# Turning the attention's tiles in two row tiles of 64 tokens, each with a PSUM bank of its own

## The chip, the cores and the metric

One Trainium2 chip, one of its cores. The time is the device time of one launch in microseconds (us). The kernel's engines are called PE (TensorE, with PEld for its weight loads), DVE (VectorE), ACT (ScalarE), POOL (GpSimd) and SP (SyncE, which only issues transfers here).

## What is computed

For 2048 tokens of width 448 the reference mixes two branches, token by token, with a gate `g`. Branch A is linear attention with 16 heads of 28; branch B sends each token to two of eight experts.

```python
g = sigmoid((x * gate_w).sum(-1))
# A
q, k, v = split(x @ wqkv)                              # 16 heads of 28
phi_q = concat(softmax(q @ w_phi), softmax(-(q @ w_phi)))   # 56 per head; phi_k alike
kv, z = phi_k^T v, sum(phi_k)
a = concat_heads(phi_q kv / (phi_q z + 1e-6)) @ wo
# B
top 2 of x @ w_gate -> gates;  b = sum over the two: gate * (silu(x @ w1[e]) @ w2[e])
out = g * a + (1 - g) * b
```

## The kernel before

The tokens are cut into 16 tiles `t` of 128. A first stage (to about 113 us) makes the values, the key maps and the state `kv` of all tiles, and routes the tokens. The stage that the change touches runs from 113 to 217 us: a loop over `t = 0 .. 17`, in which tile `t` is attended, tile `t + 2` prepared, tile `t - 1` turned, tile `t - 2` projected, and the queries of tile `t + 7` asked for. After it the experts run on PE to the end.

Order on PE, DVE and ACT is that of the program; on POOL nearly every instruction is chained behind the one before it (`in_turn`). One round `t` issues, in this order:

- POOL: three scatters of routing records (`store`, L475, in rounds 2 to 6, fewer in others), each allowed once tile `t` is attended; from round 8 on gathers of the first expert's tokens (L796) instead. Then `drop` (L586: queries' exponents less their maximum), `weigh`'s sum `om(t)` (L906) and the copy of its last 64 columns (L908). From round 9 on, a rearrangement of gathered tokens (L855).
- PE: `attend(t)` (L885, 64 matmuls in four tiles of 64x64, output `n` in the one pair of banks "T"); `flip(t + 2)`: the 128 x 1024 map of the queries is turned by eight full transposes (L712, `et`), the maps' tile `t + 2` being attended two rounds later; `project(t - 2)` (11 matmuls of 448 columns, `ao`); `turn(t - 1)`: the tile's output `om` of 128 x 512 is turned by four full transposes (L915, `ot`); `ask(t + 7)` (11 matmuls, `pq`, up to round 8); in rounds 10 to 14 `first_tokens` turns one tile of the first expert's tokens by four transposes (L860, `xgt`).
- DVE: `tops` (L581, maxima of the queries; in rounds 10 and 11 it stands behind `weigh` instead); `weigh(t)` (L895 to L901, ending in `w`, which also frees the banks of `n`); the rest of `turn(t - 1)` (L139, L140, which make `oh`, `ol`); the rest of `first_tokens` (L828, L829).
- ACT: signs and exponential of queries, the two copies of `et` (L713), the row's output `aos` (L925), `oh` (L137), `xgh` (L824).

PSUM has eight banks: "A" two (`pq`, `ao`), "T" two as one pair, "O" four in rotation (`et`, `ot`, `xgt`, and the routing's `pp`). `route(1)`, a routine that routes the second half of the tokens, advances by some steps at the head of each round; its matmuls into `pp` (L452, L454) are issued in round 1 and what reads them (L458 to L470) in round 2. L470 makes the addresses of the scatters that begin in round 2.

Of the kernel before, what the change touches and what calls it, by code (L numbers as in the profile page):

```python
# [8 lines left out]
F32 = mybir.dt.float32  # L9
# [3 lines left out]
AF = mybir.ActivationFunctionType  # L13
ALU = mybir.AluOpType
AX = mybir.AxisListType
PSUM = bass.MemoryType.PSUM
DRAM = bass.MemoryType.DRAM

P = 128
# [6 lines left out]
NT = S // P  # L26
# [36 lines left out]
LANDING = ("x00", "w0", "x10", "x20", "x30", "w1", "x01", "x40", "x11", "x50", "x21", "w2", "x31", "w3", "x41", "x51")  # L63
PIECES = ("00", "10", "20", "30", "01", "40", "11", "50", "21", "02", "12", "22", "31", "41", "03", "13", "23",
          "32", "51", "42", "52", "33", "43", "53")
BANKS = {"A": 2, "O": 4}
XLP = range(3, 16)
QBUFS = 5
ASKS = {9: 0, 10: 1, 11: 2, 12: 3, 14: 4}
# [2 lines left out]
NJ = 8  # L72
# [10 lines left out]
def gated_mix(ctx: ExitStack, tc: tile.TileContext, xt, xq, wk, wq, wv, wphi, wo, w12, out):  # L83
    nc = tc.nc
# [2 lines left out]
    cst = ctx.enter_context(tc.tile_pool(name="cst", bufs=1))  # L87
    dram = ctx.enter_context(tc.tile_pool(name="dram", bufs=1, space=DRAM))
    ps = ctx.enter_context(tc.tile_pool(name="ps", bufs=1, space=PSUM))

    def bank(tag, name):
        return ps.tile([P, 512], F32, tag=tag, name=name, bufs=BANKS[tag])

    def two_banks(name):
        return ps.tile([P, NJ, P], F32, tag="T", name=name, bufs=1)

    def after(i, others):
        for o in others:
# [37 lines left out]
    def xsplit(xh, xl, src, eng):  # L136
        nc.scalar.activation(xh, src, AF.Copy)  # L137
        lo = xh[64:P, 3]
        for i in (eng.tensor_tensor(out=lo, in0=src[64:P, 3], in1=lo.bitcast(F32), op=ALU.subtract),  # L139
                  eng.tensor_tensor(out=xl, in0=src[:, 0:3], in1=xh[:, 0:3].bitcast(F32), op=ALU.subtract)):  # L140
            if eng is nc.gpsimd:
                in_turn(i)
# [74 lines left out]
    ident = cst.tile([P, P], F32, name="ident")  # L217
# [10 lines left out]
    for what in LANDING:  # L228
        t = int(what[1])
# [41 lines left out]
    for t in range(NT):  # L271
        pool = pe if t < NT // 2 else px
# [3 lines left out]
    for n, m in (("k", D), ("v", VG), ("q", D), ("o", D)):  # L276
        pool = px if n in "qo" else pb
# [9 lines left out]
    half = [slice(64 * a, 64 * a + 64) for a in range(2)]  # L287
# [65 lines left out]
    for what in LANDING:  # L353
        t = int(what[1])
# [3 lines left out]
        c = FIRST[int(what[2])]  # L358
# [38 lines left out]
    def route(r):  # L397
        n = GROUPS[r + 1] - GROUPS[r]

        def tl(shape, name, dt=F32):  # L400
            return pr.tile([P] + shape, dt, tag=name, name=f"{name}{r}")

        tt, ts_ = nc.vector.tensor_tensor, nc.vector.tensor_scalar
        ts = slice(GROUPS[r], GROUPS[r + 1])
        b3 = [P, n, E]

        def wide(x):
            return x.unsqueeze(2).to_broadcast(b3)

        def each(x):  # L410
            return x.unsqueeze(1).to_broadcast(b3)


        def highest(l, m, sel):
            t = tl([n, E], "t")
            f = tl([n], "f")
            nc.vector.tensor_reduce(out=m, in_=l, axis=AX.X, op=ALU.max)
            tt(out=t, in0=l, in1=wide(m), op=ALU.is_equal)
            tt(out=t, in0=t, in1=each(down), op=ALU.mult)
            yield  # L420
            nc.vector.tensor_reduce(out=f, in_=t, axis=AX.X, op=ALU.max)
            tt(out=sel, in0=each(down), in1=wide(f), op=ALU.is_equal)

        l8 = L[:, ts, 0:E]
        g = gt[:, ts]
        omg, m1, m2 = tl([n], "omg"), tl([n], "m1"), tl([n], "m2")
        sel = [tl([n, E], f"sel{k}") for k in range(2)]
        l2 = tl([n, E], "l2")
        selb = tl([n + 1, E], "selb", BF16)
        nc.scalar.activation(g, L[:, ts, 8], AF.Exp, scale=-1.0)  # L430
        yield from highest(l8, m1, sel[0])
        nc.vector.scalar_tensor_tensor(out=l2, in0=sel[0], scalar=-3e38, in1=l8, op0=ALU.mult, op1=ALU.add)
        yield
        yield from highest(l2, m2, sel[1])
        nc.vector.memset(selb[:, n], 0.0)
        tt(out=selb[:, 0:n], in0=sel[0], in1=sel[1], op=ALU.add)
        tt(out=m2, in0=m2, in1=m1, op=ALU.subtract)
        yield
        nc.scalar.activation(m2, m2, AF.Exp)
        nc.vector.tensor_scalar_add(g, g, 1.0)  # L440
        nc.vector.reciprocal(g, g)
        ts_(omg, g, -1.0, 1.0, op0=ALU.mult, op1=ALU.add)
        yield
        nc.vector.tensor_scalar_add(m1, m2, 1.0)
        nc.vector.reciprocal(m1, m1)
        tt(out=rec[:, ts, 0, 1], in0=m1, in1=omg, op=ALU.mult)
        tt(out=rec[:, ts, 1, 1], in0=rec[:, ts, 0, 1], in1=m2, op=ALU.mult)
        yield
        pp = bank("O", f"pp{r}")
        nn = (n + 1) * E  # L450
        pos_p = pp[:, 0:nn].rearrange("p (t e) -> p t e", e=E)
        nc.tensor.matmul(pp[:, 0:nn], before, selb.rearrange("p t e -> p (t e)"), start=True, stop=False)  # L452
        for t in range(n):
            nc.tensor.matmul(pos_p[:, t + 1:], ones_b, selb[:, t:t + 1, :].to_broadcast([P, n - t, E]),  # L454
                             start=False, stop=t == n - 1)
        yield
        pos = tl([n + 1, E], "pos")
        tt(out=pos, in0=pos_p, in1=base.unsqueeze(1).to_broadcast([P, n + 1, E]), op=ALU.add)  # L458
        nc.vector.tensor_copy(base, pos[:, n])
        pos = pos[:, 0:n]  # L460
        slot = tl([n, E], "slot")
        s1 = tl([n, E], "s1")
        tt(out=slot, in0=pos, in1=each(kst), op=ALU.add)
        yield
        slot_f = tl([n, 2], "slot_f")
        slot_i = pr.tile([P, n, 2], I32, name=f"slot_i{r}")
        for k in range(2):
            tt(out=s1, in0=sel[k], in1=slot, op=ALU.mult)
            nc.vector.tensor_reduce(out=slot_f[:, :, k], in_=s1, axis=AX.X, op=ALU.add)
        nc.vector.tensor_copy(slot_i, slot_f)  # L470
        stores.extend((slot_i[:, t, k:k + 1], rec[:, ts.start + t, k, :]) for t in range(n) for k in range(2))
# [117 lines left out]
    def lower(e, n, pool):  # L589
        drop(e, tops(e, n, pool))  # L590
# [74 lines left out]
    for t in range(NT):  # L665
# [19 lines left out]
        if 1 <= t < 5:  # L685
            c = t - 1
# [16 lines left out]

    et = {}

    def flip(t):
        et[t] = pt.tile([P, NJ, P], F32, tag="et", name=f"et{t}", bufs=2)
        e = EQ[t].rearrange("p h f -> p (h f)")
        for a in range(0, NJ, 4):
            tp = bank("O", f"et{t}{a}")  # L710
            for j in range(4):
                nc.tensor.transpose(tp[:, j * P:(j + 1) * P], e[:, (a + j) * P:(a + j + 1) * P], ident)  # L712
            nc.scalar.activation(et[t][:, a:a + 4], tp.rearrange("p (a n) -> p a n", n=P), AF.Copy)  # L713
# [16 lines left out]
    b = blocks(kvs)  # L730
# [120 lines left out]
    def first_tokens(c):  # L851
        m = P if c < nm else EX
        t = xg[0, c][0:m]
        x4 = pm.tile([P, 4, 4, 32], F32, tag="xt", name=f"x40{c}")[0:m]
        in_turn(nc.gpsimd.tensor_copy(x4, t.rearrange("p a (c k) -> p c a k", c=4)))  # L855
        yield
        tp = bank("O", f"xgt0{c}")
        v = tp[:, 0:4 * m].rearrange("p (c n) -> p c n", c=4)
        for i in range(4):
            nc.tensor.transpose(v[:, i], x4[:, i].rearrange("p a k -> p (a k)"), ident[0:m, 0:m])  # L860
        if c == 0:
            xg[0] = (pw.tile([P, 4, CAP], F32R, tag="xgh", name="xgh0", bufs=1),
                     pw.tile([P, 3, CAP], F32R, tag="xgl", name="xgl0", bufs=1))
        at = slice(c * P, c * P + m)
        both(xg[0][0][:, :, at], xg[0][1][:, :, at], v)
# [6 lines left out]
    om, oh, ol = {}, {}, {}  # L872
# [34 lines left out]
                                        in0=w5[:, :, :, 0], in1=w5[:, :, :, 1], op=ALU.add))  # L907
        in_turn(nc.gpsimd.tensor_copy(o[:, D:512], o[:, 384:D]))  # L908

    def turn(t):  # L910
        oh[t] = pc.tile([P, 4, P], F32R, tag="oh", name=f"oh{t}")
        ol[t] = pc.tile([P, 3, P], F32R, tag="ol", name=f"ol{t}")
        tp = bank("O", f"ot{t}").rearrange("p (c n) -> p c n", n=P)
        for c in range(4):
            nc.tensor.transpose(tp[:, c], om[t][:, c * P:(c + 1) * P], ident)  # L915
        xsplit(oh[t], ol[t], tp, nc.vector)

    def project(t):
        o = bank("A", f"ao{t}")
# [244 lines left out]
    def fill_in():  # L1164
        n = len(fill)
        fill.append((*FILL[n // 2], n % 2))
        first(*fill[-1])

    def part_way():
        for g in list(coming):  # L1170
            if next(g, 0) == 0:
                coming.remove(g)

    at, k = None, 0
    for t in range(NT + 2):
        u = t + QAHEAD
# [22 lines left out]
        k = t - (NT if at is None else at)  # L1199
# [7 lines left out]
            weigh(t, n_)  # L1207
        if u < NT and not early_top:
            lower(EQ[u], f"q{u}", pr)
        if t + 2 < NT:  # L1210
            flip(t + 2)
        if t >= 2:
            if t == NT + 1:
                fill_in()
            leave_row(t - 2, project(t - 2))
        if t == NT:
            fill_in()
        if 1 <= t <= NT:
            turn(t - 1)
        if t in QASKS:  # L1220
            ask(QASKS[t], some=(0 if t else 5, 11))
        if t == NT - 1:
# [16 lines left out]
        if SPLIT <= t < SPLIT + 3 and splits:  # L1239
            if next(splits[0], 0) == 0:  # L1240
                del splits[0]
                if splits:
                    next(splits[0])
    assert not coming and not splits
    runs["on"] = False
    pc_stack.close()
    px_stack.close()
# [14 lines left out]
    for s in range(E * NFC):  # L1262
        e, fc = divmod(s, NFC)
        k, i = divmod(s, 2)
# [26 lines left out]
        n = 3 * nm  # L1291
        if e == E - 1 and fc > NFC - LATE:
            n = n // 2 if fc < NFC - 1 else 0
        if fc % 2 == 0:
            f = first_pair(e, fc // 2)
# [7 lines left out]
    with tc.manual_schedule(engines={mybir.EngineType.PE}):  # L1303
        last = reached["pe"]
        for cs in ((0, 1), (2,), (3,)):
            for at in (0, 2):
                for c in cs:
                    for i in range(2):
                        share(E - 1, NFC - LATE + at + i, c, last)
                    if at:  # L1310
                        leave(E - 1, (c,))
    pf_stack.close()


    loads, (n_ov,) = nc.values_load_multi_w_load_instructions(nov_i[0:1, 0:1], min_val=0, max_val=MAXOV)  # L1315
# [98 lines left out]
```

## Time and profile before

| | |
|---|---|
| three runs | 789.95, 790.08, 791.45 us; median 790.08 |
| the profiled execution | 790.2 us, its span 788.2 us (2.0 us lie around the span) |
| busy share of the span | PE 99%, PEld 92%, DVE 61%, POOL 43%, ACT 39% |
| stage of the change | 113.4 to 217 us of the span |

A busy share is a mean over stages. A row of a timeline gives the start in us, the duration in us of the instruction (or, for neighbours of one kind that were merged, from the first start to the last end), engine, line, operation, the tile written `<-` the tiles read, shapes (stationary partitions * columns, then the moving operand) and count; in brackets stands the idle time before it and what ended it. Matmuls overlap: what one costs is the distance between starts, not its duration.

### The profile page before, as it was taken

To read this page: it belongs to the slowest core of one execution; us is meant where nothing else is said; L and a number is where in the kernel's file an instruction comes from. 1 tells how busy PE (TensorE), PEld (TensorE's weight loads), DVE (VectorE), ACT (ScalarE), POOL (GpSimd) and SP (SyncE) were. 2 spreads that over 40 slices of the span, in tenths; PEclk is the share of its full clock that TensorE was granted. 3 is DMA by queue.
4 is the path that set the end of the run, shared out by engine and by line. 5 is a ranking of instruction groups with operands and counts; after the bars stand their busy time and mean duration, and the time that the engine had idled before them with its cause. 6 is when DMAs were issued, how large, how long until landed. Compare 5 with 4: busy or idle time off the path is not lost. (4 is left out here: it accounts for less than half of the span.)

```text
span 788.2 us, 18163 instructions
## 1 busy us (share of the span) xinstructions
PE 777.1 (99%) x7378; PEld 721.4 (92%) x7378; DVE 483.4 (61%) x1045; ACT 308.9 (39%) x523; POOL 339.9 (43%) x334
## 2 busy tenths in 40 slices
PE   8999999999999999999999999999999999999996
PEld 6888888989999999998999799999999999999995
DVE  4698978658684866574566345554754555475431
ACT  5543455556532433343334223333433333243221
POOL 4667878886223316423450147144325405423003
PEclk9999999999999999999999999999999999999999
DMA  8420000135253337324543264364345336435403
GB/s 280 121 86 1 2 2 26 38 54 180 98 170 90 111 105 164 127 94 97 144 139 109 63 144 147 112 154 130 123 120 153 129 125 157 137 129 115 134 2 46
DMA packets 39786, 85.92 MB, mean 109 GB/s; under 512 B 11312, under 2 KB 20928, under 8 KB 39700
## 3 DMA queue, kind: packets, MB, share of 16 engines
q1 hardware_dynamic: 29332, 67.88, 26.3%
q0 software_dynamic: 10224, 16.61, 11.3%
q8 instruction: 59, 0.97, 0.5%
q10 hardware_dynamic: 144, 0.23, 0.1%
q14 instruction: 27, 0.22, 0.1%
HBM read 71.89 MB, written 12.82 MB: 107 GB/s over the span
## 5 line engine op out<-in xcount | busy, mean ns | idle before, releaser
L1088 PE MATMUL acc<-w2h,hx 64*128 64x448 f32 (+2 forms) x1088 | 193.1, 363 | 0.1
L1037 ACT ACTIVATE hs<-hp 128x272 f32<-128x272 f32 (+4 forms) x154 | 70.8, 483 | 306.5 <-issue 185.8
L804 POOL DMA_INDIRECT xg<-in_xq_dram,idq x114 | 126.2, 1107 | 148.7 <-PE hp L125 52.3
L1043 DVE CAST hx<-hs 128x504 fp32r<-128x504 f32 (+5 forms) x154 | 55.5, 361 | 204.1 <-ACT hs L1037 204.0
L1088 PEld LDWEIGHTS acc<-w2h,hx 64*128 64x128 f32 (+2 forms) x1088 | 161.3, 182 | 4.9 <-ACT y L1141 1.6
L1088 PE MATMUL acc<-w2l,hx 64*128 64x448 f32 (+3 forms) x544 | 157.9, 363 | 0.0
L1004 PE MATMUL hp<-xgh,w1h 64*128 64x504 f32 (+2 forms) x490 | 149.3, 386 | 0.0
L1004 PE MATMUL hp<-xgh,w1l 64*128 64x504 f32 (+2 forms) x490 | 149.1, 385 | 0.0
L1004 PE MATMUL hp<-xgl,w1h 64*128 64x504 f32 (+2 forms) x490 | 148.8, 384 | 0.0
L960 POOL DMA_INDIRECT out_dram<-y,tabm x32 | 52.4, 1637 | 172.2 <-DVE y L1143 163.7
L1122 PE MATMUL acc<-w2h,hx 128*128 128x448 f32 (+2 forms) x366 | 111.6, 365 | 0.0
L1088 PEld LDWEIGHTS acc<-w2l,hx 64*128 64x128 f32 (+3 forms) x544 | 96.9, 182 | 1.4
L1004 PEld LDWEIGHTS hp<-xgh,w1h 64*128 64x128 f32 x490 | 87.9, 184 | 3.3 <-issue 0.3
L1004 PEld LDWEIGHTS hp<-xgh,w1l 64*128 64x128 f32 x490 | 88.1, 185 | 3.0
L1004 PEld LDWEIGHTS hp<-xgl,w1h 64*128 64x128 f32 x490 | 88.0, 184 | 3.0
L1046 DVE TENSOR_TENSOR hx<-hs,hx 128x276 fp32r<-128x276 f32 (+5 forms) x168 | 84.9, 512 | 5.3
L125 PE MATMUL hp<-xgh,w1h 128*128 128x272 f32 (+1 forms) x336 | 87.8, 289 | 0.0
L125 PE MATMUL hp<-xgh,w1l 128*128 128x272 f32 (+1 forms) x336 | 87.7, 289 | 0.0
L773 DVE TENSOR_TENSOR w1l<-wr,w1h 128x1024 fp32r<-128x1024 f32 x56 | 68.2, 1218 | 11.0 <-ACT w1h L771 10.0
L1122 PEld LDWEIGHTS acc<-w2h,hx 128*128 128x128 f32 (+2 forms) x366 | 68.0, 186 | 6.2 <-issue 0.7
L1122 PE MATMUL acc<-w2l,hx 128*128 128x448 f32 (+2 forms) x190 | 69.4, 365 | 0.0
L125 PEld LDWEIGHTS hp<-xgh,w1h 128*128 128x128 f32 x336 | 63.3, 188 | 0.6
(231 smaller groups left out, 1415.1 us busy)
## 6 DMA issues: line engine op xcount, KB each, us to landing
wr<-in_w_dram SPq DMA_DIRECT2D x56, 512.0 KB, 3.6
wr<-in_w_dram SPq DMA_DIRECT2D x46, 448.0 KB, 4.4
kept<-in_w_dram SPq DMA_DIRECT2D x10, 448.0 KB, 4.3
out_dram<-aos SPq DMA_DIRECT2D x16, 224.0 KB, 3.9
xr<-in_xt_dram SPq DMA_DIRECT2D x10, 256.0 KB, 4.5
xg<-in_xq_dram,idq POOLq DMA_INDIRECT x114, 2.7
xr<-in_xt_dram SPq DMA_DIRECT2D x6, 192.0 KB, 4.2
out_dram<-zero SPq DMA_DIRECT2D x5, 224.0 KB, 5.2
```

What stands on the lines that cost most here:

```text
L125: reached["pe"] = nc.tensor.matmul(o, a, b, start=i == 0, stop=i == n - 1)
L773: nc.vector.tensor_tensor(out=l, in0=raws[s][layer - 1], in1=h.bitcast(F32), op=ALU.subtract)
L804: i = nc.gpsimd.indirect_dma_start(out=t[:, b], out_offset=None, in_=xq, in_offset=bass.IndirectOffsetOnAxis(ap=idq[:, e, 4 * c + b:4 * c ...
L960: return nc.gpsimd.indirect_dma_start(out=out, out_offset=bass.IndirectOffsetOnAxis(ap=idx_ap, axis=0), in_=y, in_offset=None, compute_op= ...
L1004: meet(("first", i), a, lambda: nc.tensor.matmul(o[i], l, r, start=n == 0, stop=n == len(rounds) - 1), n == 0)
L1037: nc.scalar.activation(hs[:, tsl], hp, AF.Silu)
L1043: nc.vector.tensor_copy(h[:, tsl], hs[:, tsl])
L1046: nc.vector.tensor_tensor(out=h[:, a + o:b + o], in0=hs[:, a:b], in1=h[:, a:b].bitcast(F32), op=ALU.subtract)
L1088: meet((e, c), a, lambda: nc.tensor.matmul(acc[e][c][:l.shape[1], 0:D], l[half[a]], r[half[a]], start=new, stop=ends and c not in of[k + 1 ...
L1122: i = nc.tensor.matmul(acc[e][c][:l.shape[1], 0:D], l, r, start=fc == 0 and k == 0, stop=fc == NFC - 1 and k == len(pr) - 1)
```

## The change

PSUM is shared out anew for the loop over `t`: the four banks "O" become two "O" and a pair "U" that exists once; behind the loop the old shares return. `flip(t + 2)` in rounds 0 to 13 makes 16 transposes of 64 tokens instead of eight of 128: tokens 0 to 63 stand in the upper half of PE's rows and go to one bank, 64 to 127 in the lower half and go to the other, each transposed against a 64 x 64 identity. ACT still copies `et` out in two instructions of 512 elements. `turn(t - 1)` in rounds 1 to 13 does the same with eight transposes into the pair "U", and stands right behind `flip`, ahead of `project(t - 2)`, on PE and on ACT; the last three turns stay as they were. `first_tokens` and the `pp` of `route(1)` write into "U" too, and `route(1)` no longer pauses between the matmuls into `pp` and their readers, so that L458 to L463 come in round 1.

```diff
-BANKS = {"A": 2, "O": 4}
+BANKS = {"T": 1, "O": 4}
+IN_ROWS = {"T": 1, "U": 1, "O": 2}
...
+    banks = {"A": (ps, 2)}
+
+    def share_out(name, bufs):
+        if "stack" in banks:
+            banks["stack"].close()
+        banks["stack"] = ExitStack()
+        pool = banks["stack"].enter_context(tc.tile_pool(name=name, bufs=1, space=PSUM, reuse_waits="tile"))
+        banks.update({tag: (pool, n) for tag, n in bufs.items()})
...
+    def two_banks(name, tag="T"):
+        pool, n = banks[tag]
+        return pool.tile([P, NJ, P], F32, tag=tag, name=name, bufs=n)
...
-        pp = bank("O", f"pp{r}")
+        pp = two_banks(f"pp{r}", "U").rearrange("p j n -> p (j n)") if r else bank("O", f"pp{r}")
...
-        yield
+        if r == 0:
+            yield
         pos = tl([n + 1, E], "pos")
...
-    def flip(t):
+    def flip(t, rows=False):
...
+        if rows:
+            tp = [bank("O", f"et{t}{a}").rearrange("p (j n) -> p j n", j=NJ) for a in range(2)]
+            for j in range(NJ):
+                for a, k in enumerate(half):
+                    nc.tensor.transpose(tp[a][:, j], e[k, j * P:(j + 1) * P], ident[k, k])
+            for a, k in enumerate(half):
+                nc.scalar.activation(et[t][:, :, k], tp[a], AF.Copy)
+            return
...
-        tp = bank("O", f"xgt0{c}")
+        tp = two_banks(f"xgt0{c}", "U").rearrange("p j n -> p (j n)")
...
+        tp = two_banks(f"ot{t}", "U").rearrange("p (a c) (b n) -> p a (c b) n", a=2, b=2)
         for c in range(4):
-            nc.tensor.transpose(tp[:, c], om[t][:, c * P:(c + 1) * P], ident)
-        xsplit(oh[t], ol[t], tp, nc.vector)
+            for a, k in enumerate(half):
+                nc.tensor.transpose(tp[:, a, c], om[t][k, c * P:(c + 1) * P], ident[k, k])
+        xsplit(*(x.rearrange("p c (a n) -> p c a n", a=2) for x in (oh[t], ol[t])),
+               tp[:, :, 0:4].rearrange("p a c n -> p c a n"), nc.vector)
...
+    share_out("ps1", IN_ROWS)
     at, k = None, 0
     for t in range(NT + 2):
...
-        if t + 2 < NT:
-            flip(t + 2)
+        rows_too = t + 2 < NT
+        if rows_too:
+            flip(t + 2, True)
+            if t >= 1:
+                turn(t - 1, True)
         if t >= 2:
...
             leave_row(t - 2, project(t - 2))
...
-        if 1 <= t <= NT:
-            turn(t - 1)
+        if 1 <= t <= NT and not rows_too:
+            turn(t - 1, False)
...
+    share_out("ps2", BANKS)
```

## Rows read from the trace of the kernel before

**Rows 1.** The page: busy us of each engine, its share of the span and its instructions.
```profile
PE 777.1 (99%) x7378; PEld 721.4 (92%) x7378; DVE 483.4 (61%) x1045; ACT 308.9 (39%) x523; POOL 339.9 (43%) x334
```

**Rows 2.** Busy time by stretch of the loop (up to round 9, and rounds 10 to 14): length, then busy us (instructions) of each engine, the clock granted, the DMA engines' share and GB/s.
```profile
113.40:176.90 63.50, 62.69 (x949) 55.92 (x949) 46.60 (x107) 36.31 (x66) 50.72 (x54) 1.00 0.16 35
176.90:202.50 25.60, 25.29 (x448) 22.92 (x447) 20.64 (x50) 15.98 (x29) 14.88 (x20) 1.00 0.43 153
```

**Rows 3.** Timeline of PE, round 6, from its first matmul of `attend` to that of round 7.
```profile
151.01 1.16 PE L885 MATMUL n<-B,et 64*64 64x60 f32 x64
152.10 1.09 PE L712 MATMUL et<-ident,eq 128*128 128x128 f32 x8
152.95 0.45 PE L125 MATMUL ao<-WHo,oh 128*128 128x448 f32 x1
...
155.27 0.60 PE L915 MATMUL ot<-ident,om 128*128 128x128 f32 x4
155.63 0.45 PE L642 MATMUL pq<-WHq,XH 128*128 128x448 f32 x1
...
158.03 1.16 PE L885 MATMUL n<-B,et 64*64 64x60 f32 x64
```

**Rows 4.** Timeline of POOL over the same time: `om(5)`, then the scatters, `drop` and `om(6)` of round 6.
```profile
151.92 1.15 POOL L906 TENSOR_TENSOR om<-w 128x448 f32<-128x448 f32 x1
153.13 0.24 POOL L908 COPY om<-om 128x64 f32<-128x64 f32 x1
153.85 0.99 POOL L475 DMA_INDIRECT tabd<-rec,slot_i  x1 [0.48 <-issue]
...
157.43 1.72 POOL L586 TENSOR_TENSOR eq<-eq,mxq 128x896 f32<-128x896 f32 x1
159.09 1.16 POOL L906 TENSOR_TENSOR om<-w 128x448 f32<-128x448 f32 x1
```

**Rows 5.** Timeline of PE in narrow windows: the first two and the first three transposes of a `flip`; then the first three and all four of the last `first_tokens`, which turns 40 tokens. A row's duration runs to the end of its last instruction, so two rows differ by the step from one transpose to the next.
```profile
152.10 0.44 PE L712 MATMUL et<-ident,eq 128*128 128x128 f32 x2
152.10 0.55 PE L712 MATMUL et<-ident,eq 128*128 128x128 f32 x3
201.75 0.38 PE L860 MATMUL xgt<-ident,x 40*128 40x40 f32 x3
201.75 0.44 PE L860 MATMUL xgt<-ident,x 40*128 40x40 f32 x4
```

**Rows 6.** Timeline of PE, where a later stage begins to use two row tiles: the first pair of matmuls and the second.
```profile
433.65 0.49 PE L1004 MATMUL hp<-xgh,w1h 64*128 64x504 f32 x2
433.98 0.39 PE L1004 MATMUL hp<-xgh,w1l 64*128 64x504 f32 x2
```

**Rows 7.** Timeline of PE, where that stage goes back from two row tiles to the whole array: the last matmul in row tiles, the first two of the whole array.
```profile
770.20 0.38 PE L1004 MATMUL hp<-xgl,w1h 64*128 64x488 f32 x1
770.51 0.47 PE L1122 MATMUL acc<-w2h,hx 128*128 128x448 f32 x1
770.82 0.36 PE L1122 MATMUL acc<-w2l,hx 128*128 128x448 f32 x1
```

**Rows 8.** Timelines of DVE and POOL in round 2: first and last of what reads `pp`, and the first scatter behind it.
```profile
122.28 0.22 DVE L458 TENSOR_TENSOR pos<-pp,base 128x72 f32<-128x72 f32 x1
...
124.27 0.17 DVE L470 CAST slot_i<-slot_f 128x16 int32<-128x16 f32 x1
125.21 1.00 POOL L475 DMA_INDIRECT tabd<-rec,slot_i  x1 [1.86 <-PE et L712]
```

**Rows 9.** Timeline of POOL: `om(9)`.
```profile
178.25 1.17 POOL L906 TENSOR_TENSOR om<-w 128x448 f32<-128x448 f32 x1
179.49 0.23 POOL L908 COPY om<-om 128x64 f32<-128x64 f32 x1
```

**Rows 10.** Timeline of PE: the end of round 10 and the beginning and end of round 11.
```profile
181.59 0.60 PE L860 MATMUL xgt<-ident,x 128*128 128x128 f32 x4
182.12 1.16 PE L885 MATMUL n<-B,et 64*64 64x60 f32 x64
...
186.81 0.60 PE L860 MATMUL xgt<-ident,x 128*128 128x128 f32 x4
187.34 1.16 PE L885 MATMUL n<-B,et 64*64 64x60 f32 x64
```

**Rows 11.** Timelines of ACT (one row) and DVE from the `xgt` of round 10 to the `turn` of round 11.
```profile
182.36 0.60 ACT L824 ACTIVATE xgh<-xgt 128x512 fp32r<-128x512 f32 x1
183.42 0.29 DVE L828 TENSOR_TENSOR xgh<-xgt,xgh 64x128 fp32r<-64x128 f32 x1
183.73 0.56 DVE L829 TENSOR_TENSOR xgl<-xgt,xgh 128x384 fp32r<-128x384 f32 x1
184.20 0.35 DVE L895 RECIPROCAL r<-n 128x32 f32<-128x32 f32 x1
...
185.63 1.09 DVE L901 TENSOR_TENSOR w<-n,r 128x896 f32<-128x896 f32 x1
186.64 1.08 DVE L581 TENSOR_REDUCE mxq<-eq 128x32 f32<-128x896 f32 x1
...
188.07 0.56 DVE L140 TENSOR_TENSOR ol<-ot,oh 128x384 fp32r<-128x384 f32 x1
```

**Rows 12.** Timeline of PE: the last `attend`.
```profile
202.55 1.16 PE L885 MATMUL n<-B,et 64*64 64x60 f32 x64 [0.36 <-DVE w L901]
```

More of the change, by code (lines that the diff above doesn't have):

```diff
@@ L89, in gated_mix @@
     ps = ctx.enter_context(tc.tile_pool(name="ps", bufs=1, space=PSUM))
-    def bank(tag, name):
-        return ps.tile([P, 512], F32, tag=tag, name=name, bufs=BANKS[tag])
-    def two_banks(name):
-        return ps.tile([P, NJ, P], F32, tag="T", name=name, bufs=1)
+    banks = {"A": (ps, 2)}
[5 more added lines that the diff above has]
+        banks.update({tag: (pool, n) for tag, n in bufs.items()})
+    def bank(tag, name):
+        pool, n = banks[tag]
+        return pool.tile([P, 512], F32, tag=tag, name=name, bufs=n)
+    def two_banks(name, tag="T"):
+        pool, n = banks[tag]
+        return pool.tile([P, NJ, P], F32, tag=tag, name=name, bufs=n)
+    share_out("ps0", BANKS)
     def after(i, others):
@@ L908, in weigh, with turn @@
         in_turn(nc.gpsimd.tensor_copy(o[:, D:512], o[:, 384:D]))
-    def turn(t):
+    def turn(t, rows):
         oh[t] = pc.tile([P, 4, P], F32R, tag="oh", name=f"oh{t}")
         ol[t] = pc.tile([P, 3, P], F32R, tag="ol", name=f"ol{t}")
-        tp = bank("O", f"ot{t}").rearrange("p (c n) -> p c n", n=P)
+        if not rows:
+            tp = bank("O", f"ot{t}").rearrange("p (c n) -> p c n", n=P)
+            for c in range(4):
+                nc.tensor.transpose(tp[:, c], om[t][:, c * P:(c + 1) * P], ident)
+            xsplit(oh[t], ol[t], tp, nc.vector)
+            return
+        tp = two_banks(f"ot{t}", "U").rearrange("p (a c) (b n) -> p a (c b) n", a=2, b=2)
         for c in range(4):
-            nc.tensor.transpose(tp[:, c], om[t][:, c * P:(c + 1) * P], ident)
-        xsplit(oh[t], ol[t], tp, nc.vector)
+            for a, k in enumerate(half):
+                nc.tensor.transpose(tp[:, a, c], om[t][k, c * P:(c + 1) * P], ident[k, k])
+        xsplit(*(x.rearrange("p c (a n) -> p c a n", a=2) for x in (oh[t], ol[t])),
+               tp[:, :, 0:4].rearrange("p a c n -> p c a n"), nc.vector)
     def project(t):
@@ L1312, in gated_mix @@
     pf_stack.close()
+    ctx.push(banks["stack"])
     loads, (n_ov,) = nc.values_load_multi_w_load_instructions(nov_i[0:1, 0:1], min_val=0, max_val=MAXOV)
```

## Prediction, made before the changed kernel was run

> **What bounds the kernel now.** The page comes first [rows 1]: PE is busy for 99% of the span, DVE and POOL far less, so a microsecond saved on PE looks like a microsecond of the kernel. The change lies in one stage, though, so the table by stretches comes next [rows 2]. Up to round 9 PE is busy for 62.7 of 63.5 us, but POOL is busy for 50.7, at twice its mean share, and its gaps have still to be looked at. In rounds 10 to 14 PE is at 25.3 of 25.6 us and DVE at 20.6. The granted clock is 1.00, that is the level of 2.4 GHz.
>
> So the timelines decide. PE's [rows 3]: round 6 lasts 158.03 - 151.01 = 7.02 us: attend 1.09, flip 0.85 to the first `ao` row, projection 2.32, turn 0.36, queries 2.40, with no idle time. POOL's over the same time [rows 4]: from the end of `om(5)` (151.92 + 1.15 = 153.07) to the end of `om(6)` (159.09 + 1.16 = 160.25) it takes 7.18 us, and in between it is never free for longer than 0.48 us, the gap ahead of a scatter. POOL is thus the slower of the two by 0.16 us a round, and what hides it is where `turn` stands: `turn(5)` begins at 155.27 [rows 3], 2.20 us after the sum `om(5)` and 1.90 after its copy [rows 4].
>
> **What the transposes cost.** A third full transpose adds 0.55 - 0.44 = 0.11 us [rows 5]: 0.872 for the eight of `flip`, 0.436 for `turn`'s four (at 0.109). The nearest thing to a transpose of 64 tokens is that of 40, in the last `first_tokens`: a fourth adds 0.06 us [rows 5]. Two row tiles at work together are seen in the experts: their first pair of matmuls lasts 0.49 instead of 0.39 [rows 6], one weight load's 0.10 for both of them, not 0.20, so the loads of the two halves run side by side, as the matmuls do. I take 0.061 for a pair of 64-token transposes: flip 8 x 0.061 = 0.49, turn 4 x 0.061 = 0.24, a gain of 0.38 and 0.19. The bounds: the halves of a full transpose, 0.055 a pair, below; two of 0.061 one after the other, 0.122, above.
>
> The Trainium skill's page "TensorE: Matmul & The Clock Gate", section "LDWEIGHTS (loading the stationary operand)", speaks against the change: a load takes its columns divided by 1.2 GHz, however few rows it has. These transposes still load 128 columns, so by that rule a pair would be held at an estimated 0.107 and nothing gained. The rows disagree for transposes: the 40-token ones load 128 columns too and follow each other at 0.06 [rows 5].
>
> Going back from row tiles to the whole array costs something. The last matmul in row tiles starts at 770.20; by PE's 0.21 a matmul (eleven `ao` in 2.32 [rows 3]) it leaves at 770.41, while the next but one starts at 770.82, so that the first really ran from 770.61 [rows 7]: 0.20 us. Entering from `attend` costs as before, since `attend` runs in tiles of its own already. A round with both parts thus saves PE 0.38 + 0.19 - 0.20 = 0.37 us. Thirteen rounds (1 to 13), and round 0 with 0.18, are 5.0 us, if PE set the pace throughout.
>
> **Where that gain stops: POOL.** `turn(t - 1)` would now be wanted at 152.10 + 0.06 (first load) + 0.49 = 152.65 in round 6, while `om(5)` ends at 153.07 [rows 3, 4]. PE is in order: project, the queries and the next attend wait behind it, and POOL's scatters and `drop` take no less time for it. So in rounds 4 to 7 the rounds last POOL's 7.18. What PE can win there is what POOL is moved forward by. One edit does that: L458 to L463 come a round earlier, so the scatters of round 2, which start 0.77 after the addresses are done (124.27 + 0.17 to 125.21), no longer stand behind three instructions of DVE, 123.25 - 122.28, about 0.95 us [rows 8]. In round 1 they stand ahead of `weigh(1)` instead and delay it by about 0.6, and the scatters also need `attend(2)`. I take 0.45 earlier; the bounds are 0 and 0.95. Nothing else in POOL's chain up to round 9 depends on PE closely enough to count: the gathers of rounds 8 and 9 need tables that are loaded after the last scatter has landed.
>
> So `om(9)`, which ends at 179.42 [rows 9], ends at 178.97; `turn(9)` waits for it in round 10, and its last two transposes for the copy, until 179.42; plus 0.20, the projection's 2.25, it is 181.87 when PE comes to `xgt`: before, 181.59 [rows 10]. **After ten rounds PE is 0.28 us behind**, all its gain spent on waiting, since the projection now stands behind the wait and not ahead of it.
>
> **A new wait: the pair "U".** `turn(t - 1)` and `xgt` share it, so `xgt` waits until DVE has read the turned tile for the last time (L140). Before, four rotating banks kept them apart. DVE reads in program order, `weigh(t)` first. In round 11 L828 and L829 follow `xgt`: it starts at 181.87, lands 0.61 later (0.44 and latency), ACT's copy takes 0.60, and with 0.05 of handing over DVE's two take 0.85: L895 starts near 184.0 (184.20 before). From L895 to the end of L140 the row is 188.63 - 184.20 = 4.43 us, with L581 in between [rows 11]. So `xgt` can start at 188.45 instead of 186.81 [rows 10]: **+1.65**. PE, which attends from 181.87 + 0.44 + 0.09 = 182.40, comes to it after 1.09 + 0.55 + 0.24 + 0.20 + 2.25 = 4.33, at 186.73, and stands for 1.7 us, with nothing behind it allowed to pass.
>
> In rounds 12 and 13 L581 is gone (4.43 - 1.03 = 3.40). `xgt` to `xgt` is then 0.61 + 0.60 + 0.05 + 0.80 + 3.40 + 0.05 = 5.5 us against 186.81 - 181.59 = 5.22 [rows 10]: +0.28 each, giving +2.2. In round 14 nothing is turned ahead of the projection; the last attend waits for `w` as it did [rows 12], and from `xgt` 3 (199.5) by the same sum w ends near 204.2: attend at 204.3 instead of 202.55, **+1.75**. Behind it PE is full in both, so this goes to the end.
>
> Costed at nothing: the copies of `et` and `oh` and DVE's two read as many elements as before, and `et` is needed two rounds later. `aos` moves behind `oh` on ACT, the row's store on SP with it; ACT is busy for 36 of 63.5 us [rows 2], and three buffers hold the row; without that cover it is one ACT instruction, 0.6 us, a round. Two "O" banks are enough for a flip a round. Sharing out PSUM anew falls where attend waits for `kv` anyway; without cover one copy, 0.6.
>
> **Sum.** The profiled execution took 790.2 us (span 788.2 and 2.0 around it); +1.8 gives 792.0, and as the median of three was 0.1 below it, I predict **791.9 us**. A change under 0.2%, 1.6 us, is no change that this kernel's measurement can tell.
>
> **Rivals.**
> 1. The new waits as above, 791.0 to 793.4 with the bounds on POOL's shift (0 gives +2.2, 0.95 gives +1.3): 0.50. A quarter of that lies within 0.2%.
> 2. The other side: `xgt` does not wait for DVE. The point that decides is whether L140 ends ahead of PE's 4.33 us after attend; DVE's program order speaks against it (attend's results come 1.2 after its start, then 3.4). Then rounds 11 to 13 keep 3 x 0.37 of gain on +0.28, and -1.2 with the last wait for `w` met earlier: 788.9. 0.13, two thirds of it within 0.2%.
> 3. POOL gives way, because its gaps ahead of scatters (0.48 in the row) shrink, and PE's gain of rounds 2 to 10 arrives as well: about 3.2 in all with rival 2, 786.9, at most the 5.0: 785. Against it: the row ends that gap by "issue", by nothing that POOL waited for [rows 4]. 0.09.
> 4. The halves do not gain: transposes of the two row tiles follow one another, or a pair is held by its loads. At 0.109 a pair nothing is saved and 0.20 a round lost: 0.20 x 13 = 2.6 and the bank's wait of rounds 11 to 13, about 1.8: +4.4, 794.5. At 0.122 another 8 x 0.013 + 4 x 0.013 = 0.16 a round in the ten where PE then leads, near +6: 796. The page's rule above gives 794.4. The 0.49 of [rows 6] and the 0.06 of [rows 5] speak against it. 0.17.
> 5. The change is hidden altogether, waits and gains, near 790: 0.08. Something dearer than any of this, above 796: 0.03.
>
> **Chances.** Faster by over 0.2%: 0.09 and a third of 0.13, 0.13. Within: 0.12 + 0.09 + 0.08 and rounding, 0.30. Slower: 0.38 + 0.17 + 0.03, about 0.57. The range from 788.7 to 796.0 takes in cases 1, 2, 4 and 5 and leaves out 3, part of 2 and the last, under 2 in 10; the likeliest case alone is 791.0 to 793.4.
>
> **What would show it.** Flip's step should be 0.06 a pair, and 0.2 should lie between `ot` and `ao`. PE should be idle ahead of `ot` by `om` (some 0.3 us in rounds 4 to 7, over 1 us in round 10), and ahead of `xgt` by `ol` (1.7 us in round 11, 0.6 in 12 and 13). The last attend should start 1.75 late. I am wrong if `xgt` follows `ao` without a gap, if POOL's round gets shorter than 7.1, or if the step of a pair is near 0.11.

## The result, and the profile after

The changed kernel takes **795.02 us** (median of six, 794.61 to 797.20) against 790.14 for the kernel before in the same company (six runs): ratio 1.0064, interval 1.0051 to 1.0078. It is slower by 4.9 us, where +1.8 was forecast. The profiled execution took 796.1 us, its span 794.2. The page's first part shows that PE works as long as before [rows 1]; the span is longer because it stands:

```profile
PE 776.9 (98%) x7542; PEld 713.5 (90%) x7542; DVE 486.0 (61%) x1045; ACT 309.8 (39%) x523; POOL 340.6 (43%) x334
```

Executions differ by up to 2 us in when the loop begins (`attend(0)` at 113.45 before, 114.28 after, 113.0 to 115.0 in the runs below), so places in the loop are counted from `attend(0)` here. `attend(15)` starts 202.55 - 113.45 = 89.10 us behind it before [rows 12] and 207.87 - 114.28 = 93.59 after: +4.49. Behind it nothing is lost or won: the last matmul ends 667.07 and 671.58 us behind `attend(0)`, +4.51.

What the edit itself does is as forecast. Timeline of PE in round 8, where the tile to turn has long been there, up to the first matmul of round 9:

```profile
167.78 1.16 PE L907 MATMUL n<-B,et 64*64 64x60 f32 x64
168.87 0.71 PE L727 MATMUL et<-ident,eq 64*128 64x64 f32 x16
169.42 0.41 PE L944 MATMUL ot<-ident,om 64*128 64x64 f32 x8
...
174.41 1.16 PE L907 MATMUL n<-B,et 64*64 64x60 f32 x64
```

Sixteen transposes of 64 tokens take 169.42 - 168.87 = 0.55 us, a first load and eight steps of 0.061; in full transposes it was 0.85 [rows 3]. The round takes 174.41 - 167.78 = 6.63 us, where one of the same parts took 7.02 before [rows 3]. And here is where it goes, PE's waits in the loop added up (time, number of waits, longest):

```profile
PE ot L944 <- POOL om L928: 3.1, 6, 1.1
PE xgt L882 <- DVE ol L153: 2.3, 3, 1.4
PE n L907 <- DVE pos L472: 0.9, 1, 0.9
PE n L907 <- DVE w L923: 0.7, 1, 0.7
```

The third line is the wait of `attend(1)`, which comes 118.60 - 114.28 = 4.32 us behind `attend(0)`; it came 117.70 - 113.45 = 4.25 behind it before, so this wait is not new. Of the rest, only 0.16 us for `om` in round 1 stood there before.

The first line in round 6, on PE and then on POOL, which answer to [rows 3] and [rows 4]:

```profile
153.44 1.16 PE L907 MATMUL n<-B,et 64*64 64x60 f32 x64
154.53 0.71 PE L727 MATMUL et<-ident,eq 64*128 64x64 f32 x16
155.40 0.57 PE L944 MATMUL ot<-ident,om 64*128 64x64 f32 x8 [0.16 <-POOL om L928]
```
```profile
154.20 1.15 POOL L928 TENSOR_TENSOR om<-w 128x448 f32<-128x448 f32 x1
...
156.13 0.99 POOL L489 DMA_INDIRECT tabd<-rec,slot_i  x1 [0.48 <-PE ot L944]
...
161.37 1.15 POOL L928 TENSOR_TENSOR om<-w 128x448 f32<-128x448 f32 x1
```

`om(5)` ends at 155.35 and the turn starts 0.05 us later; POOL's round is 161.37 - 154.20 = 7.17 us, its gap ahead of the scatter 0.48, both as before. The second line of the list, in rounds 10 and 11, on PE and then on DVE, beside [rows 10]:

```profile
182.16 0.57 PE L944 MATMUL ot<-ident,om 64*128 64x64 f32 x8 [1.10 <-POOL om L928]
...
185.05 0.63 PE L882 MATMUL xgt<-ident,x 128*128 128x128 f32 x4
...
191.71 0.63 PE L882 MATMUL xgt<-ident,x 128*128 128x128 f32 x4 [1.43 <-DVE ol L153]
```
```profile
191.00 0.56 DVE L153 TENSOR_TENSOR ol<-ot,oh 128x384 fp32r<-128x384 f32 x1
```

`ol(10)` ends at 191.56 and `xgt` starts 0.15 us behind it, as forecast, but `xgt` of round 10, forecast 181.87 - 113.45 = 68.42 us behind `attend(0)`, comes 185.05 - 114.28 = 70.77 behind it. The loss that was not forecast, 2.35 us, is thus older than round 10. DVE shows it in rounds 1 and 2, with POOL's instructions of the same time in the second fence, beside [rows 8] and [rows 9]:

```profile
118.63 2.23 DVE L473 COPY base<-pos 128x8 f32<-128x8 f32 x1
120.78 0.21 DVE L477 TENSOR_TENSOR slot<-pos,kst 128x64 f32<-128x64 f32 x1
...
123.33 1.09 DVE L923 TENSOR_TENSOR w<-n,r 128x896 f32<-128x896 f32 x1
...
126.53 0.17 DVE L484 CAST slot_i<-slot_f 128x16 int32<-128x16 f32 x1
...
130.95 3.00 DVE L506 TENSOR_TENSOR more<-base 128x64 f32<-128x64 f32 x1
```
```profile
118.01 1.72 POOL L600 TENSOR_TENSOR eq<-eq,mxq 128x896 f32<-128x896 f32 x1
119.67 1.15 POOL L928 TENSOR_TENSOR om<-w 128x448 f32<-128x448 f32 x1
...
127.47 1.00 POOL L489 DMA_INDIRECT tabd<-rec,slot_i  x1 [1.53 <-PE ot L944]
...
180.97 1.14 POOL L928 TENSOR_TENSOR om<-w 128x448 f32<-128x448 f32 x1
```

A copy of eight columns takes 2.23 us and ends at 120.86; POOL's `om` ends at 120.82, after two of its instructions in a row. So `w(1)` ends 10.14 us behind `attend(0)`. Before, it ended 8.00 behind it:

```profile
120.36 1.09 DVE L901 TENSOR_TENSOR w<-n,r 128x896 f32<-128x896 f32 x1
```

`attend(2)` waits for it (the last line of the list), DVE comes later to the addresses, and the first scatter, again 0.77 us after they are done, comes 13.19 behind `attend(0)` instead of 11.76: 1.43 later where 0.45 earlier was forecast.

### The profile page after: what moved, and what is told of

Read it like the earlier page. It is cut to its first block, busy times and chain, and to the rows that moved or that the text cites. A ratio compares the mean times of both kernels' runs of the same rounds, so it can differ in the third digit from the quotient of the medians.

```text
span 794.2 us, 18486 instructions
## 1 busy us (share of the span) xinstructions
PE 776.9 (98%) x7542; PEld 713.5 (90%) x7542; DVE 486.0 (61%) x1045; ACT 309.8 (39%) x523; POOL 340.6 (43%) x334
## 5 line engine op out<-in xcount | busy, mean ns | idle before, releaser
L1118 PE MATMUL acc<-w2l,hx 64*128 64x448 f32 (+3 forms) x544 | 159.5, 363 | 0.0
```

The source lines that it names most:

```text
L1118: meet((e, c), a, lambda: nc.tensor.matmul(acc[e][c][:l.shape[1], 0:D], l[half[a]], r[half[a]], start=new, stop=ends and c not in of[k + 1 ...
```

## Experiments

Theory: the 4.5 us are (a) `xgt`'s stand for the pair U and (b) the readers of `pp`, moved to where DVE is held up by POOL; without both the change is worth about nothing, since the early turn puts PE behind POOL. Rivals: the row tiles or the earlier turn lose by themselves, or the two causes hide each other. All times were taken beside the kernel before. Four kernels ran on a chip where that took 795.85 us, at a mean granted clock of 0.992 to 0.997 instead of 0.996 to 0.999; so the ratios are compared.

| kernel | us | before, us | ratio and interval | `attend(15)` behind `attend(0)` |
|---|---|---|---|---|
| before | | 790.14 | | 89.10 |
| changed | 795.02 | 790.14 | 1.0064 (1.0051 to 1.0078) | 93.59 |
| changed, again | 795.19 | 790.20 | 1.0055 (1.0041 to 1.0069) | 93.53 |
| base from PSUM | 794.34 | 790.18 | 1.0056 (1.0042 to 1.0069) | 93.53 |
| xgt in A | 791.19 | 790.18 | 1.0010 (1.0001 to 1.0019) | 90.07 |
| the two together | 791.01 | 790.18 | 1.0013 (1.0004 to 1.0022) | 90.09 |
| flips alone | 789.55 | 790.18 | 0.9991 (0.9982 to 1.0000) | 87.74 |
| order alone | 791.02 | 790.20 | 1.0007 (0.9998 to 1.0016) | 89.62 |
| all readers from PSUM | 799.36 | 795.85 | 1.0039 (1.0022 to 1.0057) | 91.94 |
| pause kept | 799.17 | 795.85 | 1.0037 (1.0024 to 1.0051) | 92.35 |
| pause kept, xgt in A | 796.29 | 795.85 | 1.0000 (0.9988 to 1.0012) | 88.71 |
| the last, with the turn late, in row tiles | 796.32 | 795.85 | 1.0002 (0.9990 to 1.0014) | 88.36 |
| row tiles where nothing waits | 788.91 | 790.20 | 0.9984 (0.9975 to 0.9993) | 86.51 |

**xgt in A.**
```diff
-        tp = two_banks(f"xgt0{c}", "U").rearrange("p j n -> p (j n)")
+        tp = bank("A", f"xgt0{c}")
```


> The changed kernel, in which first_tokens writes its transposes into a bank of the pair A, and no longer into U. Theory (xgt waits for DVE's last read of the turned tile): PE stands no longer ahead of xgt in rounds 11 to 13, each of these rounds takes 1.4 us (round 11) and 0.7 us (12, 13) less than in the changed kernel, the last attend starts about 3.2 us earlier, and the time falls by about 3.2 us, to about 792. Rival (the rounds are late because DVE's chain or POOL's om is late anyway, and the bank only shows it): the wait moves to another instruction of PE and the time falls by less than 1 us.

Measured 791.19 us, 3.5 us earlier at `attend(15)`. PE at the end of round 10 and of round 11:
```profile
184.24 0.60 PE L882 MATMUL xgt<-ident,x 128*128 128x128 f32 x4
...
189.08 0.60 PE L882 MATMUL xgt<-ident,x 128*128 128x128 f32 x4
```
`xgt` follows `xgt` in 4.84 us with no wait, where the changed kernel needs 6.66 and the kernel before 5.22 [rows 10]. Cause (a) is shown.

**Base from PSUM**, and both together.
```diff
-        nc.vector.tensor_copy(base, pos[:, n])
+        tt(out=base, in0=pos_p[:, n], in1=base, op=ALU.add)
```


> The changed kernel, in which the routing's running counts (base) are renewed from PSUM and their old value, not copied from a tile in SBUF. Theory (the copy waits until POOL's two running tensor instructions end, 2.23 us in the profile of the changed kernel, and delays weigh(1), attend(2) and the first scatter of round 2): the instruction takes about 0.2 us; the first scatter of round 2 starts 2 us earlier against attend(0) than in the changed kernel (11.2 instead of 13.2 us after it), om(9) about 2 us earlier, and the time falls by 1.8 to 2.2 us, to about 793. Rival (the 2.23 us come from what the instruction is or from the fresh input, and round 2's lateness from the shared banks): the instruction or the one behind it still takes about 2 us and the time stays within 0.5 us of 795.

> The changed kernel with both edits: base renewed from PSUM, and first_tokens' transposes in a bank of A. Theory (two separate waits, added up): 5.2 us less than the changed kernel, about 789.8, so 0.5 to 1.5 us less than before. Rival (one wait hides behind the other): 791.5 to 793.

Both missed; of the rival, the sentence on the instruction behind came out. DVE, and POOL's `om` of the time:
```profile
117.29 0.17 DVE L473 TENSOR_TENSOR base<-pp,base 128x8 f32<-128x8 f32 x1
117.37 2.27 DVE L477 TENSOR_TENSOR slot<-pos,kst 128x64 f32<-128x64 f32 x1
```
```profile
118.41 1.14 POOL L928 TENSOR_TENSOR om<-w 128x448 f32<-128x448 f32 x1
```
The instruction that was mended takes 0.17, and the next one, which reads SBUF twice, takes 2.27 and ends at 119.64, `om` at 119.55. The wait belongs to no one instruction; it falls on the first copy or sum that takes all its inputs from SBUF. So both were changed.

**All readers from PSUM.**
```diff
...
+        if r == 0:
...
+            tt(out=first_slot, in0=base, in1=kst, op=ALU.add)
+        else:
+            tt(out=slot, in0=pos_p[:, 0:n], in1=each(first_slot), op=ALU.add)
+            tt(out=base, in0=pos_p[:, n], in1=base, op=ALU.add)
```


> The changed kernel, but in routing round 1 no VectorE instruction of the part that was moved takes all its inputs from SBUF: the sum of base and the experts' first slots is made once, in round 0, the slots are then pos_p (PSUM) plus that sum and the new base is pos_p (PSUM) plus base; the tile pos is not made. Theory (the one that waits is whichever VectorE instruction reads SBUF alone while GpSimd's eq/om instructions run): the 2.2 us that the copy of base took in the changed kernel, and the slots' sum in the experiment before, is gone altogether; the two instructions take 0.2 us each, weigh(1) ends about 2.1 us earlier than in the changed kernel, attend(2) starts 0.6 to 0.9 earlier (TensorE is next), the first scatter of round 2 0.9 to 1.4 earlier, and the time falls by 0.9 to 1.6 us, to 793.4 to 794.1. Rival (the place in the round delays, not where the operands lie): some instruction of the two takes about 2 us again and the time stays within 0.4 us of 795.0.

```profile
118.75 0.23 DVE L481 TENSOR_TENSOR slot<-pp,first_slot 128x64 f32<-128x64 f32 x1 [0.19 <-PE pp L468]
118.89 0.16 DVE L482 TENSOR_TENSOR base<-pp,base 128x8 f32<-128x8 f32 x1
118.97 1.07 DVE L600 TENSOR_REDUCE mxq<-eq 128x32 f32<-128x896 f32 x1
```
```profile
118.19 1.71 POOL L605 TENSOR_TENSOR eq<-eq,mxq 128x896 f32<-128x896 f32 x1
...
125.88 1.00 POOL L494 DMA_INDIRECT tabd<-rec,slot_i  x1 [1.53 <-PE et L732]
```
The wait is gone, with POOL at work as before. (In round 2 it comes back shorter: the first product of two SBUF tiles, L487, takes 0.84 us and ends 0.09 after an `om`; its second one takes 0.22.) The first scatter comes 125.88 - 114.46 = 11.42 us behind `attend(0)`: 0.34 earlier than in the kernel before, near the 0.45 of the prediction, and 1.77 earlier than in the changed kernel, more than the 0.9 to 1.4 expected. `attend(15)` gains 1.65 us; by the ratios it is 0.16 to 0.25 per cent, 1.3 to 2.0 us, though their intervals overlap a little. Cause (b) is shown by the trace, and that it is the operands' place that decides.

**Pause kept**, then with `xgt` in A too.
```diff
-        pp = two_banks(f"pp{r}", "U").rearrange("p j n -> p (j n)") if r else bank("O", f"pp{r}")
+        pp = bank("A" if r else "O", f"pp{r}")
...
-        if r == 0:
-            yield
+        yield
```


> The changed kernel with the routing pause put back (the readers of pp run in round 2 as in the kernel before; pp then takes a bank of A, as it may not hold the pair U or a bank of O over the pause). Theory (the move of pp's readers into round 1 put them behind GpSimd and delayed weigh(1), attend(2) and the first scatter): attend(2) starts within 0.2 us of the kernel before's 9.44 after attend(0), the first scatter at 11.8 instead of 13.2, and the time falls by 1.2 to 2.0 us against the changed kernel, to 793.0 to 793.8; the stand for the pair U in rounds 11 to 15 remains. Rival (the delay in rounds 1 and 2 is the row tiles' or the earlier turn's): attend(2) stays near 10.3, and the time within 0.4 us of 795.0.

> Both repairs at once: the pause kept (pp in a bank of A) and xgt in a bank of A instead of the pair U. Theory (the loss has these two causes and they add): 795.0 less 3.8 (measured for xgt alone) less 1.2 to 2.0 gives 789.2 to 790.0; what remains of the change, row tiles and the earlier turn, is then worth 0 to 0.9 us against the kernel before. Rival (the delays overlap, one hides the other): 790.6 to 791.4, as with xgt alone.

The pause does what was expected, in the ratio too: it brings `attend(15)` forward by 1.24 us and the first scatter to 11.76. Of both repairs together the time can't tell theory from rival, since the interval (0.9988 to 1.0012) holds values of both; the trace can: `attend(15)` comes 4.88 earlier, as much as the two apart (3.52 + 1.24 = 4.76). They add, and what is left of the change is within the measurement of no change.

**The turn late, in row tiles** (behind `ao`; else as the last).


> As the experiment with both repairs, but the turn goes back behind the projection ao, where the kernel before has it, still in row tiles of 64 tokens and in the pair U. Theory (from round 3 on GpSimd's 7.18 us a round bounds the kernel only because the early turn waits for om of the round before; with the turn late TensorE needs 6.84 a round less 0.24 for the turn's row tiles plus up to 0.2 for a second way back to the whole array): rounds 3 to 9 take 6.6 to 6.85, attend(15) starts 87.0 to 88.0 us after attend(0), and the time is 787.5 to 789.6, no slower than with whole-array turns (789.55). Rival (GpSimd bounds the rounds whatever the order, over the queries' maps): rounds 3 to 9 take 7.0 to 7.2 and the time is 789.5 to 790.5.

**Flips alone**: flips in row tiles; turns whole-array, behind `ao`; pause kept; `pp` and `xgt` share a bank, the turns have another.


> Only the flips in two row tiles: turn stays in full transposes behind the projection, in a bank of its own; first_tokens and the routing's counts share another; the routing keeps its pause, so that base is copied in round 2 as before. Theory (a pair of 64-token transposes takes 0.061 us, going back to the whole array 0.20, and POOL is hidden as long as turn stands behind the projection): a round is 0.18 us shorter on PE, 14 rounds give up to 2.5 us, less what POOL's 7.18 us take back in rounds 8 to 10 and DVE at the end: 1.6 to 2.5 us less than before, about 788. Rival (PE's gain is lost wherever it is made, since POOL or DVE sets the round): within 0.6 us of before.

PE from the end of `ao` to the second matmul of the queries, first the late turn in row tiles, then the whole-array one:
```profile
148.59 0.77 PE L138 MATMUL ao<-WHo,ol 128*128 128x448 f32 x3
149.29 0.46 PE L943 MATMUL ot<-ident,om 64*128 64x64 f32 x8
...
149.99 0.36 PE L655 MATMUL pq<-WLq,XH 128*128 128x448 f32 x1
```
```profile
144.55 1.16 PE L906 MATMUL n<-B,et 64*64 64x60 f32 x64
...
148.01 0.77 PE L138 MATMUL ao<-WHo,ol 128*128 128x448 f32 x3
148.62 0.60 PE L937 MATMUL ot<-ident,om 128*128 128x128 f32 x4
...
149.26 0.37 PE L655 MATMUL pq<-WLq,XH 128*128 128x448 f32 x1
...
151.39 0.81 PE L906 MATMUL n<-B,et 64*64 64x60 f32 x40
```
149.99 - 148.59 = 1.40 us against 149.26 - 148.01 = 1.25: a turn in row tiles that needs a way in and out for itself alone is 0.15 us dearer than one in the whole array. Rounds 4 to 8 take 7.00 us each with them, and 151.39 - 144.55 = 6.84 without. So my theory of the late turn fell, and its rival too, which laid the 7.0 to POOL: in the flips' kernel PE's round of 6.84 is shorter than POOL's 7.18, since turns behind `ao` leave POOL room to fall behind; POOL has caught up by round 10, where `om(10)` waits 0.54 us for PE.

The flips' own theory missed in time: 1.6 to 2.5 us less was expected, 0.6 is measured (0 to 1.4 by the interval), so the rival's "within 0.6" is not excluded. The trace shows the gain, 0.18 a round in rounds 4 to 8, and `attend(15)` 89.10 - 87.74 = 1.36 us earlier.

**Order alone**: the turn early, flips and turns whole-array; pause kept, `pp` and `xgt` in A.


> Only the order of the change: the turn of tile t-1 stands right behind the flip of tile t+2 and has a bank of its own, but both are whole-array transposes as in the kernel before; the routing pause is kept, and pp and xgt take a bank of A. Theory (the early turn makes TensorE wait for om, so that GpSimd's 7.18 us bounds rounds 3 to 9, and the row tiles' saving is hidden behind that wait): rounds 3 to 9 take 7.1 to 7.2 us, attend(15) starts 89.1 to 89.9 us after attend(0) against 89.10 in the kernel before, and the time is 0 to 0.9 us over the kernel before. Rival (the early turn is worth something by itself, since the banks come free earlier): rounds of 6.9 to 7.0 and a time 0.5 to 1.0 us under the kernel before.

```profile
151.27 1.16 PE L906 MATMUL n<-B,et 64*64 64x60 f32 x64
152.36 1.09 PE L733 MATMUL et<-ident,eq 128*128 128x128 f32 x8
153.38 0.66 PE L937 MATMUL ot<-ident,om 128*128 128x128 f32 x4
...
158.44 0.46 PE L906 MATMUL n<-B,et 64*64 64x60 f32 x16
```
As expected in place and time: the round takes 158.44 - 151.27 = 7.17 us, POOL's, and `attend(15)` is 0.52 later than before; rounds 5 to 7 take 7.12 to 7.17, while rounds 3, 4 and 8, for which the same was expected, stay at 7.02. The flip keeps its 0.1 a transpose, and yet this round is as long as those of the changed kernel, 7.08 to 7.22 in rounds 4 to 7.

**Row tiles where nothing waits**: flips in row tiles; turns whole-array and late up to round 10, in row tiles and early in rounds 11 to 13; pause kept, `pp` and `xgt` in A.
```diff
...
-            if t >= 1:
+            if t > 10:
                 turn(t - 1, True)
...
```


> Row tiles where nothing waits: the flips in row tiles in every round; the turns whole-array and behind ao up to round 10, as in the kernel before, and in row tiles right behind the flip only in rounds 11 to 13, where om of the tile has long been there; the routing pause kept, pp and xgt in a bank of A. Theory (a row-tile group saves if it shares one way into and out of the row tiles with another and waits for nobody): rounds 3 to 9 take 6.84 as with the flips alone, rounds 11 to 13 take 4.85 instead of 5.04, attend(15) starts 86.4 to 87.4 us after attend(0) against 89.10 before, and the time is 1.7 to 2.6 us under the kernel before. Rival (something behind attend(15), as the last weigh or the transfers of the experts' weights, takes the gain back): attend(15) as early as that, but the time within 0.8 us of the kernel before.

```profile
181.51 1.16 PE L906 MATMUL n<-B,et 64*64 64x60 f32 x64
182.59 0.71 PE L726 MATMUL et<-ident,eq 64*128 64x64 f32 x16
183.15 0.42 PE L943 MATMUL ot<-ident,om 64*128 64x64 f32 x8
...
186.36 0.79 PE L906 MATMUL n<-B,et 64*64 64x60 f32 x35
187.35 0.68 PE L906 MATMUL n<-B,et 64*64 64x60 f32 x29 [0.20 <-issue]
```
Round 11 takes 186.36 - 181.51 = 4.85 us against 5.22 [rows 10], the 0.37 of the prediction. `attend(15)` and the last matmul are 2.59 us earlier than in the kernel before. The time is 1.3 us less, by the interval 0.6 to 2.0: the lowest here, though its interval overlaps that of the flips alone, and it lies between my theory's 1.7 to 2.6 and its rival. The profiled execution loses the difference ahead of `attend(0)` (114.41 instead of 113.45); one execution of each can't tell whether that is chance. The break inside `attend(12)`, put down to "issue", stands in the flips' kernel as well (0.54) and not in the others; its cause is open.

**The changed kernel again.**


> The changed kernel once more, beside the two that follow and on the chip that they run on, so that they stand against it directly. 4 to 6 us over the kernel before (0.5 to 0.8 per cent); attend(15) starts 93.4 to 93.8 us after attend(0).

It repeats in time and in the loop.

## Why the prediction was right and where it was short

The sign and the mechanism of the likeliest case (slower, by the two waits) came out, and the size did not: +1.8 forecast, +4.9 measured. The 795.0 us lie above that case's own 791.0 to 793.4. They lie inside the stated range only because it was stretched to 796.0 for rival 4, whose mechanism did not occur; that the range held is luck. By its steps, counted from `attend(0)`:

- **The transposes: right.** 0.061 a pair, 0.55 for the flip, and 0.37 a round where nothing waits: 0.39 in round 8 of the changed kernel (6.63 against 7.02), 0.37 in round 11 of the kernel with row tiles where nothing waits. The rule of the Trainium skill's page "TensorE: Matmul & The Clock Gate", section "LDWEIGHTS (loading the stationary operand)", which would have held a pair at an estimated 0.107, does not hold for these transposes. Rival 4 is out.
- **POOL stops the gain: right.** Its round stayed 7.17 and its gap 0.48, so rival 3 is out; the order alone, with no row tile at all, gives the same round.
- **POOL's shift: the term that was mis-sized, and most of the miss.** "I take 0.45 earlier; the bounds are 0 and 0.95" was one-sided. `om(9)` starts 66.69 us behind `attend(0)` instead of 64.80 [rows 9]: 1.89 later, 2.34 worse than forecast. Of this 1.43 + 0.45 = 1.88 is the first scatter. The working charged the moved instructions to `weigh(1)` at "about 0.6", their length where they stood before; at the new place POOL works on, and one of them takes 2.2 us. With no such wait (all readers from PSUM) the scatter came 0.34 early, and `om(7)` with it (49.59 against 49.93), so the step's reasoning held up to there but for that wait. The trace of before had the sign of it twice, on DVE and then on POOL:

```profile
122.54 0.55 DVE L459 COPY base<-pos 128x8 f32<-128x8 f32 x1
...
129.31 2.38 DVE L492 TENSOR_TENSOR more<-base 128x64 f32<-128x64 f32 x1
```
```profile
121.91 1.14 POOL L906 TENSOR_TENSOR om<-w 128x448 f32<-128x448 f32 x1
...
130.45 1.15 POOL L906 TENSOR_TENSOR om<-w 128x448 f32<-128x448 f32 x1
```

The same copy of eight columns ends at 123.09, `om` at 123.05; a comparison of 64 columns takes 2.38 us and ends at 131.69, `om` at 131.60.

- **"Nothing else in POOL's chain up to round 9 depends on PE closely enough to count": wrong by 0.4.** The first gather of round 8 starts 2.05 us behind `attend(8)` both before (167.13 behind 165.08) and after (169.83 behind 167.78). PE, put behind POOL by the early turn, gives the delay back to POOL there: POOL's lag grows from 1.45 at `om(7)` to 1.87 at that gather. The kernels without the first wait show this loss by itself: the gather is again 2.05 behind `attend(8)`, and with all readers from PSUM the lead of 0.34 is gone there (53.72 against 53.68 before), with the pause kept the gather is 0.44 late. With all readers from PSUM `om(9)` starts 64.85 behind `attend(0)`, against 64.80 before, so the forecast's 0.45 did not reach it even without the first wait.
- **The pair U: right.** From `xgt` to `xgt` round 11 takes 191.71 - 185.05 = 6.66 us (forecast 188.45 - 181.87 = 6.58); the last attend is 22.82 us behind `xgt` of round 10, forecast 204.3 - 181.87 = 22.43. The stand of 1.43 was forecast as 1.7. Rival 2 is out. What it costs, 3.5 us by the experiment, is more than the 22.82 - (202.55 - 181.59) = 1.86 that this stretch lost against the kernel before [rows 10, 12], because without the stand rounds 11 to 13 each keep 0.38 of gain, and the last attend's wait of 0.36 [rows 12] goes.
- **Sum.** 2.35 of the miss stood at `xgt` of round 10 and 2.74 at `attend(15)`, of the 3.1 in the time; the rest is not placed, and the interval of the ratio (4.0 to 6.2 us over before) allows for it. What was costed at nothing appears in no wait of PE's list.

## What to carry to other kernels

An instruction moved to another round is not priced by its length in the old one: look at what the other engine does at the new place, and bound the cost on both sides. A faster step ahead of a wait is worth nothing, and a wait set ahead of work that hid it hands the slower engine's pace to the one that bounds the kernel; the same row tiles gained when the turn was early only where its input had long been there. A shared single buffer is priced by the last reader in its engine's program order, not by the transfer between the two users.

## What the runs showed of the hardware

- A VectorE copy within SBUF, or an instruction with two SBUF inputs, waits until GpSimd's running elementwise instructions end, through two in a row: the copy of eight columns 2.23 us, a sum of two SBUF tiles 2.27, the comparison L506 3.00 (to 133.95, `om` to 133.86), each ending 0.04 to 0.09 us after `om`. The profile shows it as a long instruction and not as a wait, so it stands in no list of waits. The same sums with one input in PSUM took 0.16 to 0.23 us at the same place, and a reduction of 896 columns from SBUF its usual 1.07. The Trainium skill's page "SBUF — State Buffer", section "Who interferes with whom", says that a copy can take, and an instruction with two SBUF inputs takes, a port pair shared with GpSimd under an exclusive lock, and that a reduction does not; the trace agrees, and it was not weighed in the prediction.
- The way into and out of row tiles pays when it is shared: behind `attend` and a flip, a turn in row tiles saved (round 11 takes 4.85 us against 5.04 with the flips alone); between two stretches of the whole array it cost 0.15 us more than a whole-array one.
